# A linear-attention scan followed by a Fourier-mixing block: moving weight conversions, norms and three unread products around the first mixing

## The chip, the cores and the metric

The kernel runs on one core of a Trainium2 chip. The metric is the device time of one execution in microseconds, taken as the median of several runs. The engines are TensorE (PE in the profile, with its weight loads as PEld), VectorE (DVE), ScalarE (ACT), GpSimd (POOL) and SyncE (SP, which here only issues DMAs). Each engine works through its own list of instructions in order and waits on semaphores for the others.

## What is computed

The first half is a delta-rule recurrence over 768 positions for 4 batches of 8 heads with 48 elements each. Its output, laid out as (4, 768, 384), is the input x of the second half.

```
k_n = k / (norm(k) + 1e-6)
for t: y[t] = q[t] @ state
       state += beta[t] * outer(k_n[t], v[t] - k_n[t] @ state)
mixed = real(fft(fft(x, axis=positions), axis=model))
u     = x + mixed
un    = (u - mean(u)) / sqrt(var(u) + 1e-6)
out   = u + relu(un @ w_ch1) @ w_ch2
```

w_ch1 is 384 x 1536 and w_ch2 is 1536 x 384. They arrive as 64-bit floats, and the kernel makes 32-bit floats of them with integer and float operations on ScalarE and VectorE.

## The kernel before

**The scan.** Each batch is cut into six loads of 128 positions, each load into two chunks of 64. A load needs keys turned by TensorE (pre_a, L324), queries turned and multiplied with the keys (pre_q, L533), and the inverse of a small triangular system, which VectorE builds step by step for four loads at once (invert16, L460, in half-size blocks for the first three rounds; invert, L401, later). pre_m16 (L600) joins the half-size inverses: it scales Z on ScalarE, multiplies with the Gram blocks, evicts ND and MT on ScalarE, and makes three further products with a subtraction (Z, L647), an eviction and an addition (MT, L651) between them. step (L680) then carries the state over one chunk, and outputs (L744) gives x.

**The mixing.** folds (L783) adds and subtracts mirrored halves of x on VectorE. fourier (L820) first multiplies the folds with tables over positions (evt, odt), evicts the sums to F, and then, for each of six tiles of 128 rows, multiplies F with the table over the model axis (dtab), evicts one half as Q on ScalarE, adds both halves to x on VectorE, and takes mean and variance. The norms rstd = (var + 1e-6)^(-1/2) are made on GpSimd for two tiles at once (L893 to L897).

**The feed-forward part.** mlp (L900) works on three groups of two tiles. normed_of gives un on VectorE, turned transposes it on TensorE (ptr) and evicts it to unT, first_of makes twelve products ph with w1, each evicted through a Relu to hT by ScalarE, and second_of makes a product po with w2 over twelve pieces and adds it to x. The products ph, po, ptr, the position sums pf and the unread products share one pair of PSUM buffers ("post").

**The weights.** weights (L224) is a generator for both weight matrices, one after the other, each in twelve pieces of 128 x 384. A piece takes two calls: the first issues the ScalarE copy L278, the VectorE mask L279, and for the piece before, the two ScalarE steps L283 and L284; the second issues the VectorE product L291 of an earlier piece, then L295, L299 and L301, and the DMA that stages a later piece. For w1 there are two pairs of working buffers, so the product is that of the piece just before; for w2 three, so it lies two pieces back. w2's stage and working buffers are the fold buffers E and O3 of the first batch. w1's working buffers are those that later hold M (the inverse of round 2, zeroed on GpSimd at L476) and unT.

**The order.** Up to the end of the first mixing the order on PE, DVE, ACT and POOL is written out by hand: advance(gen, n) lets a generator issue up to its n-th next yield, drain lets it issue all the rest. convert(n) calls the conversion n times. In the fifth step of the scan (g = 4) the conversions stand between the state's step and the rest of pre_m16. After the first fourier sums, lines 1273 to 1300 start the feed-forward part; a loop over the twelve first products (L1284) mixes in conversions, the other tiles of the mixing, load 7's pre_m16 (ms[7]), and the remaining key turns (k1 to k3). For the next two loads (period at g = 6 and 7) only PE's order is written out, and the rest is ordered by a scheduler. period (L1002) gives each of its six slots a number of calls to the inversion (inv) and to the conversion (conv) at g = 6:

```python
            if g == NL:
                advance(inv, 4)
                advance(conv, 3 if i < 4 else 4)
```

The function spin (L1099) makes TensorE products that nobody reads; before the change it is called with three and with six, both early in the scan.

Of the kernel before, what the change touches and what calls it, by code (L numbers as in the profile page):

```python
# [64 lines left out]
def kernel(  # L65
# [155 lines left out]
    half_n = const.tile([128, GT], F32, name="half_n")  # L221
    nc.gpsimd.memset(half_n, -0.5)

    def weights():  # L224

        if moe_w_ch1.dtype == F32:
            nc.sync.dma_start(out=w1, in_=moe_w_ch1.rearrange("(c p) f -> p c f", p=128))
            nc.sync.dma_start(out=w2, in_=moe_w_ch2.rearrange("(c p) m -> p c m", p=128))  # L230
            return
        w1v = moe_w_ch1.bitcast(I32).rearrange("(c p) (f two) -> p c f two", p=128, two=2)
        w2v = moe_w_ch2.bitcast(I32).rearrange("(c p) (m two) -> p c m two", p=128, two=2)
        n = DM
        sets = [
            [(w1v[:, :, i:i + 128], w1[:, :, i:i + 128]) for i in range(0, DFF, 128)],
            [(w2v[:, i:i + 1], w2[:, i:i + 1]) for i in range(KF)]]
        for last, pieces in enumerate(sets):
            if last:

                E, O3 = spare.pop()
                ring = E.rearrange("p e t m -> p (e t m)").bitcast(I32).rearrange(
                    "p (i m two) -> p i m two", m=n, two=2)
                tmp = O3.rearrange("p e t m -> p (e t m)").rearrange("p (i e m) -> p i e m", e=2,
                                                                    m=n)
                tmp = [tmp[:, i] for i in range(3)]
                deep = 3
            else:
                ring = wk.tile([128, 4, n, 2], I32, tag="big", bufs=2, name="w64")
                tmp = None  # L250
                deep = 4

            def stage(i):
                if i < len(pieces):
                    src = pieces[i][0]
                    nc.sync.dma_start(
                        out=ring[:, i % deep].rearrange("p (c f) two -> p c f two",
                                                        c=src.shape[1]), in_=src)

            for i in range(deep):  # L260
                stage(i)
            yield
            if tmp is None:
                tmp = [wk.tile([128, 2, n], F32, tag="M", name="wtmp0"),
                       wk.tile([128, 2, n], F32, tag="unT", bufs=2, name="wtmp1")]

            def of(i):
                t = tmp[i % len(tmp)]
                return ring[:, i % deep, :, 0], ring[:, i % deep, :, 1], t[:, 0], t[:, 1].bitcast(I32)


            lag = len(tmp) - 1
            for i in range(len(pieces) + lag):
                if i < len(pieces):
                    lo, hi, man, num = of(i)


                    nc.scalar.activation(man, lo.bitcast(U32), ACT.Copy, scale=2.0 ** -52, bias=1.0)  # L278
                    nc.vector.tensor_scalar(num, hi, 0xFFFFF, None, op0=ALU.bitwise_and)  # L279
                if 0 < i <= len(pieces):  # L280

                    num0 = of(i - 1)[3]
                    nc.scalar.activation(num0, num0, ACT.Relu, scale=-1.0, bias=edges[:, 0:1])  # L283
                    nc.scalar.activation(num0, num0, ACT.Relu, scale=-2.0 ** 23,  # L284
                                         bias=edges[:, 1:2])
                yield
                if i >= lag:
                    _, _, man0, num0 = of(i - lag)
                    dst = pieces[i - lag][1]
                    c = dst.shape[1]  # L290
                    nc.vector.tensor_tensor(dst, man0.rearrange("p (c f) -> p c f", c=c),  # L291
                                            num0.bitcast(F32).rearrange("p (c f) -> p c f", c=c),
                                            op=ALU.mult)
                if i < len(pieces):
                    nc.vector.scalar_tensor_tensor(man, num, 2.0 ** -20, man, op0=ALU.mult,  # L295
                                                   op1=ALU.add)

                    man = man.bitcast(I32)
                    nc.vector.scalar_tensor_tensor(man, hi, -2 ** 31, man, op0=ALU.bitwise_and,  # L299
                                                   op1=ALU.bitwise_or)  # L300
                    nc.vector.tensor_scalar(num, hi, 20, 0x7FF, op0=ALU.logical_shift_right,  # L301
                                            op1=ALU.bitwise_and)
                    stage(i + deep)
                yield
# [515 lines left out]
    def fourier(b):  # L820
# [43 lines left out]
        for T in range(NC):  # L864
# [27 lines left out]
            nc.vector.bn_aggr(mv[:, tt, :], bst)  # L892
            if tt == GT - 1:  # L893
                rstd = wk.tile([128, GT], F32, tag="rstd", bufs=NC // GT, name="rstd")
                nc.gpsimd.tensor_scalar(rstd, mv[:, :, 1], 1e-6, None, op0=ALU.add)
                nc.gpsimd.tensor_tensor(rstd, rstd, half_n, op=ALU.pow)
                norms.append((mv, rstd))  # L897
            yield

    def mlp(b):  # L900
# [24 lines left out]
        def first_of(g):  # L925
            hT = hs[g] = wk.tile([128, KF, GT * 128], F32, tag="big", bufs=2, name="hT")
            for fc in range(KF):
                ph = ps_post([128, GT * 128], "ph")
                for dt in range(KD):
                    mm(ph, w1[:, dt, 128 * fc:128 * fc + 128], un[g][:, dt, :], dt == 0,  # L930
                       dt == KD - 1)
                nc.scalar.activation(hT[:, fc, :], ph, ACT.Relu)  # L932
                yield
# [14 lines left out]
        turns = [normed_of(0), turned(0), first_of(0), normed_of(1)]  # L948
# [3 lines left out]
        else:  # L952
            turns += [second_of(0, 0), turned(1), second_of(0, 1), first_of(1), normed_of(2),
# [48 lines left out]
    def period(g, side):  # L1002
# [48 lines left out]
        for i in range(SLOTS):  # L1051
# [11 lines left out]
            if g == NL:  # L1063
                advance(inv, 4)
                advance(conv, 3 if i < 4 else 4)
# [24 lines left out]
    with tc.manual_schedule(engines=engines):  # L1090
# [6 lines left out]
        unread = ps_post([128, 512], "unread")  # L1097

        def spin(n):  # L1099

            for _ in range(n):
                nc.tensor.matmul(unread[:, 0:DM], lhsT=idle[:, 0:128], rhs=idle, start=True,  # L1102
# [19 lines left out]
        conv = weights()  # L1122
# [12 lines left out]
        spin(6)  # L1135

# [15 lines left out]
        first = part(conv, 2 * KF + 2)  # L1152
        converted = 0
        fold = fd = iter(())

        def convert(n):
            nonlocal converted
            advance(first, n)
            converted += n
# [9 lines left out]
        for g in range(NL - 1):  # L1169
# [22 lines left out]
            else:  # L1192
# [20 lines left out]
                if g > 1:  # L1213
# [4 lines left out]
                fill(3)  # L1218
                if g == 4:
                    advance(n2)  # L1220
                    drain(qs[g + 1])
                    convert(1)
                elif g > 1:
                    convert(1)
                    advance(n2)
                    convert(2 if g == 3 else 1)
                else:
                    advance(n2)
                if g != 4:
# [24 lines left out]
        drain(fd)  # L1254
        drain(keys[0])
        advance(c1)
        late = outputs(g)
# [7 lines left out]
        advance(ms[6])  # L1265
        f = fourier(0)
# [86 lines left out]
```

## Time and profile before

| | |
|---|---|
| median of 3 runs | 754.34 us (752.1 to 760.21) |
| the profiled execution, whole | 761.02 us |
| its span, first to last instruction | 758.9 us |
| TensorE busy | 696.9 us (92% of the span) |
| VectorE busy | 378.6 us (50%) |
| ScalarE busy | 263.7 us (35%) |
| GpSimd busy | 69.7 us (9%) |
| mean granted TensorE clock | 0.953 |

How to read the profile: busy time is summed per engine over the span. Rows of the span in 40 slices give tenths of busy time, and for the clock tenths of full speed. In order of time, a row has its start and length in us, engine, line, operation, tile written, tile read, shape and count, and in brackets the engine's idle time before it with what ended it. A 32-bit matrix product shows as two MATMUL rows, so a count of x6 is three products. The lines below are those of the kernel before.

### The profile page before, as it was taken

What the parts mean: (1) busy time and instruction counts of PE and PEld (TensorE: products, weight loads), DVE (VectorE), ACT (ScalarE), POOL (GpSimd) and SP (SyncE); (2) the same over time, 40 slices, a digit from 0 to 9 for tenths busy, and PEclk for the clock granted to TensorE, in tenths of its full rate; (3) what the DMA queues carried; (4) which work ended last, traced back from release to release, by engine and by line L of the source; (5) the groups of instructions that cost most, each with busy time, mean ns of one, the idle gap of its engine ahead of it and who ended that gap; (6) DMA issues with size and microseconds to landing.
All of it is one profiled execution on the core that took longest, in us unless ns stands there. A gap on an engine that the chain in (4) does not pass through costs nothing.

```text
span 758.9 us, 23039 instructions
## 1 busy us (share of the span) xinstructions
PE 696.9 (92%) x10170; PEld 538.0 (71%) x10170; DVE 378.6 (50%) x957; ACT 263.7 (35%) x644; POOL 69.7 (9%) x114
## 2 busy tenths in 40 slices
PE   6877879598989987999999999999999999999998
PEld 4677868476767655877857767868667678777684
DVE  5867776669932499433198327278512240600000
ACT  5544663568623321223422323223223221211120
POOL 7000000100000011001110210020100110100000
PEclk8698797799999999999999999999999999999999
DMA  9842352014312322002222211001220000000000
GB/s 152 215 74 41 88 135 83 18 54 124 87 29 55 60 44 44 12 11 47 52 45 48 44 34 39 1 13 42 43 44 12 13 12 0 22 1 21 11 10 22
DMA packets 111862, 36.09 MB, mean 48 GB/s; under 512 B 101873, under 2 KB 109842, under 8 KB 111762
## 3 DMA queue, kind: packets, MB, share of 16 engines
q1 hardware_dynamic: 109938, 33.86, 20.5%
q8 instruction: 80, 1.31, 0.7%
q0 software_dynamic: 640, 0.43, 0.4%
q10 hardware_dynamic: 1184, 0.33, 0.3%
q14 instruction: 20, 0.16, 0.1%
HBM read 29.88 MB, written 4.72 MB: 46 GB/s over the span
## 4 chain that ended last, share of the span: by engine, by line
PE 75%; DVE 16%; ACT 5%; issue 2%; DMA 1%; POOL 0%; DVEq 0%; ACTq 0%; POOLq 0%
PE po L110 23%; PE ph L110 21%; PE one L110 16%; PE pair L110 10%; PE one L113 2%; DVE M L452 1%; DVE tmp L448 1%; DVE w L291 1%; PE ptr L113 1%; PE unread L1102 1%; PE pf L110 1%; DMA C<-in_k_dram 1%; DVE M L522 1%; DVE Z L647 1%; DVE tmp L519 1%
## 5 line engine op out<-in xcount | busy, mean ns | idle before, releaser
L110 PE MATMUL ph<-unT,w 128*128 128x256 f32 x864 | 207.7, 392 | 2.8 <-ACT hT L932 2.0
L110 PE MATMUL po<-w,hT 128*128 128x384 f32 x576 | 205.1, 495 | 0.0
L110 PEld LDWEIGHTS ph<-unT,w 128*128 128x128 f32 x864 | 162.4, 194 | 27.6 <-ACT hT L932 2.4
L110 PEld LDWEIGHTS po<-w,hT 128*128 128x128 f32 x576 | 103.7, 190 | 56.7 <-issue 0.3
L932 ACT ACTIVATE hT<-ph 128x256 f32<-128x256 f32 x144 | 54.9, 382 | 145.0 <-PE ph L110 144.9
L943 DVE TENSOR_TENSOR x<-x,po 128x384 f32<-128x384 f32 x24 | 13.2, 550 | 107.0 <-PE po L110 107.0
L741 DVE TENSOR_TENSOR S<-S,pair 128x192 f32<-128x192 f32 x40 | 14.0, 349 | 73.9 <-PE pair L110 73.9
L110 PEld LDWEIGHTS one<-V,MT 64*64 64x64 f32 x768 | 30.5, 141 | 19.5 <-issue 9.2
L884 DVE TENSOR_TENSOR x<-x,one 128x193 f32<-128x193 f32 x24 | 8.5, 354 | 69.8 <-ACT Q L875 69.8
L110 PE MATMUL one<-V,MT 64*64 64x48 f32 x768 | 35.7, 227 | 3.6 <-DVE V L700 1.8
L452 DVE TENSOR_TENSOR M<-M,tmp 128x31 f32<-128x31 f32 (+15 forms) x93 | 34.7, 373 | 3.2
L448 DVE TENSOR_TENSOR tmp<-A,M 128x31 f32<-128x31 f32 (+15 forms) x93 | 34.2, 367 | 2.5
L110 PE MATMUL one<-MT,ND 64*64 64x64 f32 x768 | 30.4, 231 | 5.0 <-DVE x L885 2.6
L110 PEld LDWEIGHTS one<-MT,ND 64*64 64x64 f32 x768 | 27.8, 146 | 6.0 <-ACT Q L875 3.0
L700 DVE TENSOR_TENSOR V<-V,pair 128x192 f32<-128x192 f32 x33 | 11.5, 350 | 38.7 <-PE pair L110 35.4
L110 PEld LDWEIGHTS one<-dtab,F 97*128 97x128 f32 (+1 forms) x192 | 25.2, 191 | 5.2 <-ACT F L879 0.5
L110 PEld LDWEIGHTS pair<-U,K 64*64 64x64 f32 x704 | 16.6, 139 | 17.4 <-issue 14.9
L322 ACT ACTIVATE QT<-one 128x512 f32<-128x512 f32 x24 | 14.3, 594 | 38.9 <-PE one L113 38.7
L110 PE MATMUL one<-dtab,F 97*128 97x97 f32 (+1 forms) x192 | 25.9, 275 | 0.0
L110 PE MATMUL pair<-KT 48*32 48x64 f32 (+1 forms) x1152 | 21.1, 238 | 5.1 <-ACT KT L322 3.8
L110 PEld LDWEIGHTS pair<-S,KT 48*64 48x64 f32 x528 | 10.7, 133 | 20.1 <-issue 10.8
L710 ACT ACTIVATE U<-one 128x192 f32<-128x192 f32 x36 | 11.9, 330 | 37.7 <-PE one L110 37.7
(176 smaller groups left out, 1003.0 us busy)
## 6 DMA issues: line engine op xcount, KB each, us to landing
w<-in_moe_w_ch_dram SPq DMA_DIRECT2D x12, 384.0 KB, 5.6
E<-in_moe_w_ch_dram SPq DMA_DIRECT2D x12, 384.0 KB, 4.3
out_dram<-x SPq DMA_DIRECT2D x24, 192.0 KB, 1.9
K<-in_k_dram SPq DMA_DIRECT2D x92, 48.0 KB, 2.7
V<-in_v_dram SPq DMA_DIRECT2D x92, 48.0 KB, 2.2
C<-in_k_dram SPq DMA_DIRECT2D x18, 192.0 KB, 9.3
Q<-in_q_dram SPq DMA_DIRECT2D x18, 192.0 KB, 3.1
w<-in_q_dram SPq DMA_DIRECT2D x6, 192.0 KB, 7.5
```

The costliest lines, as they stand in the source:

```text
L110: nc.tensor.matmul(o, lhsT=lhsT, rhs=rhs, start=start, stop=stop, skip_group_check=True)
L113: nc.tensor.matmul(o, lhsT=src, rhs=ident[0:src.shape[0], 0:src.shape[0]], is_transpose=True, start=start, stop=True, skip_group_check=True)
L291: nc.vector.tensor_tensor(dst, man0.rearrange("p (c f) -> p c f", c=c), num0.bitcast(F32).rearrange("p (c f) -> p c f", c=c), op=ALU.mult)
L322: nc.scalar.activation(dst.rearrange("p h j t -> p (h j t)"), pt, ACT.Copy)
L448: nc.vector.tensor_tensor(t, A[:, j + 1:W, j:j + 1].broadcast_to([128, n, j + 1]), M[:, j:j + 1, 0:j + 1].broadcast_to([128, n, j + 1]), o ...
L452: nc.vector.tensor_tensor(M[:, j + 1:W, 0:j + 1], M[:, j + 1:W, 0:j + 1], t, op=ALU.add)
L700: nc.vector.tensor_tensor(R4, R4, pw[:, :, 0:2 * D].rearrange("p a (j e) -> p a j e", e=D), op=ALU.subtract)
L710: nc.scalar.activation(U.rearrange("p j e -> p (j e)"), pu[:, 0:4 * D], ACT.Copy)
L741: nc.vector.tensor_tensor(s1v, s0.rearrange("p h j e -> p h (j e)"), pk, op=ALU.add)
L884: nc.vector.tensor_tensor(near, near, pb[:, 0, 0:MH + 1], op=ALU.add)
L932: nc.scalar.activation(hT[:, fc, :], ph, ACT.Relu)
L943: nc.vector.tensor_tensor(x[:, T, :], x[:, T, :], po, op=ALU.add)
```

## The change

1. The generator for both weights becomes weight(last), one for each matrix. w2's first three stage DMAs are issued by the hand-written part ahead of the loop over first products, and w1's remaining calls and w2's are joined by chain(conv, w2s).
2. In the scan's step g = 4, two conversion calls move from ahead of the rest of pre_m16 (and of its subtraction Z) to behind it, and the fold steps there are dropped to be drained later, behind the last chunk's step.
3. In the first mixing, one conversion call no longer stands between the eviction of F and the first Q. ms[7] starts ahead of the position sums. Load 7's first two products of pre_m16 are issued behind the first two mixing tiles, with two unread products between and one after them; they read the table evt.
4. The loop over first products issues two conversion calls behind each product, in place of two behind the first two and one behind the others. The mixing's other tiles are issued at products 1, 3, 6 and 9, not 1, 4, 7 and 10. The query turn for the next load, nq, is issued inside the loop.
5. un of the second group is issued within first_of(0), behind its sixth product, for the first batch; later batches keep their order.
6. The norm rstd is made for each tile by itself: two GpSimd instructions a tile, of one column, for all batches.
7. In period at g = 6, the inversion gets 5 calls a slot instead of 4, and the conversion 2 (4 in the last slot) instead of 3 or 4.

```diff
-    half_n = const.tile([128, GT], F32, name="half_n")
+    half_n = const.tile([128, 1], F32, name="half_n")
...
-    def weights():
+    def weight(last):
...
+        if last:
+            pieces = [(w2v[:, i:i + 1], w2[:, i:i + 1]) for i in range(KF)]
...
+        else:
+            pieces = [(w1v[:, :, i:i + 128], w1[:, :, i:i + 128]) for i in range(0, DFF, 128)]
...
+            if tt == 0:
+                rstd = wk.tile([128, GT], F32, tag="rstd", bufs=NC // GT, name="rstd")
+            rt = rstd[:, tt:tt + 1]
+            nc.gpsimd.tensor_scalar(rt, mv[:, tt, 1:2], 1e-6, None, op0=ALU.add)
+            nc.gpsimd.tensor_tensor(rt, rt, half_n, op=ALU.pow)
             if tt == GT - 1:
-                rstd = wk.tile([128, GT], F32, tag="rstd", bufs=NC // GT, name="rstd")
-                nc.gpsimd.tensor_scalar(rstd, mv[:, :, 1], 1e-6, None, op0=ALU.add)
-                nc.gpsimd.tensor_tensor(rstd, rstd, half_n, op=ALU.pow)
                 norms.append((mv, rstd))
...
                 nc.scalar.activation(hT[:, fc, :], ph, ACT.Relu)
+                if b == 0 and g == 0 and fc == 5:
+                    drain(normed_of(1))
                 yield
...
-        turns = [normed_of(0), turned(0), first_of(0), normed_of(1)]
+        turns = [normed_of(0), turned(0), first_of(0)]
...
-            turns += [second_of(0, 0), turned(1), second_of(0, 1), first_of(1), normed_of(2),
+            turns += [normed_of(1), second_of(0, 0), turned(1), second_of(0, 1), first_of(1), normed_of(2),
...
             if g == NL:
-                advance(inv, 4)
-                advance(conv, 3 if i < 4 else 4)
+                advance(inv, 5)
+                advance(conv, 2 if i < 5 else 4)
...
         def spin(n):
 
+            unread = ps_post([128, 512], "unread")
+            src = idle if idle is not None else evt[:, 0, 0:DM]
             for _ in range(n):
-                nc.tensor.matmul(unread[:, 0:DM], lhsT=idle[:, 0:128], rhs=idle, start=True,
+                nc.tensor.matmul(unread[:, 0:DM], lhsT=src[:, 0:128], rhs=src, start=True,
                                  stop=True, skip_group_check=True)
...
                 fill(3)
-                if g > 1:
+                if g > 1 and g != 4:
                     convert(2)
                 drain(nm)
                 advance(n2)
                 advance(c1)
-                fill(3)
                 if g == 4:
+                    convert(2)
                     advance(n2)
                     drain(qs[g + 1])
                     convert(1)
-                elif g > 1:
-                    convert(1)
+                else:
+                    fill(3)
+                    if g > 1:
+                        convert(1)
                     advance(n2)
-                    convert(2 if g == 3 else 1)
-                else:
-                    advance(n2)
-                if g != 4:
+                    if g > 1:
+                        convert(g - 1)
                     drain(qs[g + 1])
...
-        drain(fd)
         drain(keys[0])
         advance(c1)
+        drain(fd)
...
         advance(ms[6])
+        advance(ms[7])
         f = fourier(0)
         advance(f)
         drain(fold)
         convert(1)
         advance(f, 4)
-        convert(1)
+        w2s = weight(1)
+        advance(w2s)
         advance(f, 2)
         side, done = mlp(0), 0
+        advance(ms[7])
+        convert(1)
+        advance(side)
+        spin(2)
+        advance(ms[7])
+        spin(1)
         advance(side)
         advance(ms[6])
-        advance(ms[7])
-        advance(side)
-        convert(3)
-        advance(ms[7])
-        convert(2)
-
+
+        conv = chain(conv, w2s)
+
+        nq = pre_q(NL)
         k1, k2, k3 = keys[1:]
-        rest = [ms[6], k1, ms[7], k1, ms[7], ms[6], k2, ms[7], k2, ms[7], k3, k3]
+        rest = [k1, ms[7], k1, ms[7], k2, ms[7], k2, k3, nq, k3]
         for fc in range(KF):
-            if converted < 2 * KF + 2:
-                convert(2)
-            else:
-                advance(conv)
             advance(side)
-            if fc % 3 == 1:
+            advance(conv, 2)
+            if fc in (1, 3, 6, 9):
                 advance(f)
-            drain(rest[fc]) if fc == 5 else advance(rest[fc])
+            if fc < len(rest):
+                advance(rest[fc])
         drain(f)
-        nq = pre_q(NL)
-        advance(nq)
         for m in ms[6:] + keys[1:]:
             drain(m)
-        advance(side)
         done = 3 + KF
         inv = invert16(2)
```

## The prediction

> **What bounds the kernel now.** I read the busy slices first, then the order of time on TensorE, then a table of windows.
>
> ```profile
> PE   6877879598989987999999999999999999999998
> ...
> DVE  5867776669932499433198327278512240600000
> ACT  5544663568623321223422323223223221211120
> ...
> PEclk8698797799999999999999999999999999999999
> ```
>
> A slice is 19 us. From slice 16 on TensorE is at 9 nearly everywhere, so the later batches are bound by products that the change leaves alone. Slices 5 to 11 (95 to 228 us) are different: PE falls to 5 to 8, the clock dips, and VectorE stands at 9 to 10 in 9 and 10. The change works there. In order of time on PE, with the idle time and its releaser in brackets:
>
> ```profile
> 130.63 2.03 PE L110 MATMUL one<-dtab,F 97*128 97x97 f32 x16
> 138.56 1.54 PE L113 MATMUL ptr<-pack,un 128*128 128x128 f32 x6 [5.90 <-DVE un L911]
> ...
> 149.22 1.56 PE L110 MATMUL ph<-unT,w 128*128 128x256 f32 x6 [1.98 <-ACT hT L932]
> 153.41 1.15 PE L110 MATMUL one<-MT,ND 64*64 64x64 f32 x32 [2.62 <-DVE x L885]
> ...
> 179.97 0.70 PE L110 MATMUL pair<-QT,KT 48*64 48x64 f32 x32 [2.83 <-ACT QT L322]
> ...
> 183.37 2.86 PE L110 MATMUL ph<-unT,w 128*128 128x256 f32 x12 [0.86 <-ACT unT L922]
> ...
> 212.47 1.11 PE L110 MATMUL pair<-QT,KT 48*64 48x64 f32 x32 [3.34 <-DVE S L741]
> ```
>
> That is 17.5 us of waits. The first is the first mixing's: PE has nothing until two rows of tiles are normed. The next two stand behind a train of conversions on DVE and ACT. The last ends with VectorE's 16-step inversion (its last transpose, L527, ends at 212.2). The train waits on itself, once per conversion of a w1 piece:
>
> ```profile
> 142.49 0.56 DVE L291 TENSOR_TENSOR w<-wtmp 128x384 f32<-128x384 f32 x1 [1.06 <-ACT wtmp L284]
> ...
> 145.71 0.56 DVE L291 TENSOR_TENSOR w<-wtmp 128x384 f32<-128x384 f32 x1 [1.06 <-ACT wtmp L284]
> ```
>
> So a w1 piece takes 3.2 us (1.3 on ACT, then 1.9 on DVE) when nothing lies between. The clock, in windows of 3.41 us (columns: PE, weight loads, DVE, ACT, POOL busy, clock, DMA share, GB/s):
>
> ```profile
> 106.73:110.14 3.41, 1.48 (x55) 1.26 (x50) 3.31 (x9) 0.06 (x1) 0.00 (x0) 1.00 0.40 84
> 110.14:113.55 3.41, 2.81 (x97) 2.49 (x89) 1.51 (x4) 2.65 (x5) 0.00 (x0) 0.50 0.62 149
> ...
> 130.62:134.03 3.41, 2.04 (x17) 1.86 (x16) 0.98 (x4) 2.32 (x6) 0.00 (x0) 1.00 0.70 227
> 134.03:137.45 3.42, 0.00 (x0) 0.00 (x0) 2.71 (x9) 1.12 (x3) 0.40 (x2) 0.50 0.00 0
> ```
>
> The clock halves at 110.14 and stays so to 123.79, again from 134.03 to 144.27, from 154.51 to 157.93 and from 212.54 to 215.95, each time after a thinly used window.
>
> **Part by part.** *Fifth step of the scan (g = 4).* Two conversion steps leave the place ahead of the subtraction Z (L647). In the chain of waits they are L279 0.27, L291 0.47, L295 0.48, L299 0.56, L301 0.27: 2.07 us, and Z starts at 108.32. Its product on PE ends at 106.6, so Z moves to 106.65: 1.7 us. In exchange three fold rows (L805, L808, L810: 1.24 us) go behind the last U (L722). The folds behind that U then sum to 10.1 us (before: 117.41 to 125.84, 8.4). In this profile the window before 110.14 is used for 1.48 of 3.41 us; with Z earlier PE's 1.9 us of idle in it shrink to about 0.7, and I expect the clock to hold. The products between 110.14 and the last U shrink by 2.3 us (full-clock rows: 0.7 for 1.1, 0.65 for 1.1). The last U then comes at 117.4 - 1.7 - 2.3 = 113.4, folds end at 123.5, and the position sums, which wait for the second fold (119) and run 5.2 + 2.8 us, end at 126.9 instead of 130.6: 3.7 us. If the clock falls anyway, or did not fall before, the longer fold tail eats the 1.7: zero. Both ends are kept.
>
> Here a rule of the Trainium skill stands against the trace: "TensorE: Matmul & The Clock Gate", section "HAM oscillation — how this bites in real kernels", puts the limit at idle gaps over some 3.4 us. The longest gap before 110.14 is 1.17 us, and the clock fell. By the rule this edit is worth nothing and the three unread products below are needless; by the rows it is worth 3.7. I go by the rows. The same page's Part 1 says that the window runs freely. Every clock change here is a whole number of 3.41 us after the first one, so the trace agrees, and where a dip falls can differ between executions. That matters for the median below.
>
> *First mixing.* The conversion trio on ACT ahead of the first Q (L278, L283, L284, 1.5 us) goes: the first tile's products end at 131.65, so VectorE's first add starts at 132.0, not 133.05: 1.05 us. rstd per tile (two POOL rows, 0.22 and 0.72 before; one column has no row; between half of that and the same, I take the same) lets one un (0.47) run inside the 1.15 us wait: 0.45. So un is ready at 137.4. PE meanwhile has load 7's first product (1.15 at full clock, 1.97 before), two unread products, load 7's second (1.15), one unread product. An unread one is 128x384: 24 such po rows take 7.75 us in the chain, two rows a product, 0.65. Sum 4.25 us between 132.5 and 137, gated by ND and MT on ACT (1.4 us) and by the release of the first tile's PSUM buffer. They cost nothing while un is later; if un came sooner, at most the last 0.65 shows (1.3 at half clock). The half clock to 144.27 goes (5.7 us of PE work in it: 2.85), and 1.97 of load 7's product no longer stands between ptr and the first product ph. With ptr at 137.0 and two evictions of 0.49, ph starts at 138.5, not 141.93: 3.4 us. With the 3.7: 134.8.
>
> *The loop of 12 first products.* Before, conversion steps stood 22 ahead, 14 in it, 20 calls in the next period; now 17, 24 and 14. Sums for the new loop: DVE 12 conversions x 2.05 + 4 mixing tiles x 1.95 + un, MT, V 2.0 = 34.4 us. ACT 12 x 1.65 + 12 evictions x 0.37 + three key turns with Gram copies 7.6 + Q, mirror (1.75), MT, QT 4.1 = 35.9. PE about 27. The first five iterations are w1's ping-pong: 5 x 3.2 + 2 x 0.95 of mixing that the 1.06 us waits don't cover = 18. The other seven (w2 runs two pieces deep, so no ping-pong) are bound by ACT's remaining 21.6. Together 40 us, to 174.8; before, 34.0, to 175.9. So the conversions moved in here use up what was gained, and PE idles some 13 us in small pieces; windows this thin could again halve the clock once (1.7).
>
> *After the loop.* QT for the next load and un of the second group are now issued inside it. QT's wait (2.83) and most of unT's (0.86) go, and the way from the last ph to the second group's first ph is 2.8 us, not 7.5: 177.6 for 183.37, 5.8 us. Then PE is full up to 209.1, so it reaches the inversion at 203.3.
>
> *The inversion.* VectorE's busy time from un (138.9) to 212.2 is 60.7 us, the same work after. It starts at 137.4 - 3.7 = 133.7, with 5.6 us idle in the loop and 1 elsewhere: 201. ACT's Z and MT take 1.9 more: 203. So PE no longer waits there: 203.3 for 212.47, 9.2 us, and the half clock to 215.95 (3.41 us of PE work: 1.7) goes. Sum 10.9.
>
> *At nothing.* POOL's M memset (L476) now stands ahead of the fourth tile's rstd and waits for the eleventh w1 piece (in this trace the memset follows that L291 directly). The fourth tile's stats come 2 us later, which covers the memset's 0.98; else un and the conversions queued behind it on DVE wait 1 us. 24 more POOL rows lie on an engine 9% busy: per later batch 0.3 us won to 1 lost, I take 0. SP issues the same loads, w2's not later than before; landing is 4 to 6 us, three pieces ahead. Stalls called "issue" (about 1 us each) may shift: 1 us either way.
>
> **The profile's run and the median.** The profiled execution took 761.02 (span 758.9 and 2.1 around it), 6.7 over the median. 761.0 - 10.9 = 750.1 would be an execution as unlucky with the clock. The median one, 754.34, probably has no dip at 110, and then the 3.7 isn't there to win: 754.3 - 7.2 = 747.1; if it has, 743.4. I say 745.
>
> **Rivals.** (1) The loop meets only its ACT sum, 36 us: all later gains grow by up to 4, VectorE's end (197) allows it: 741. For it: mixing rows fill the ping-pong. Against: ACT is in order, and its evictions wait for PE. (2) Within 1%: the loop takes 44 to 46 us, because key turns and evictions (1.3 us an iteration) add to the ping-pong instead of filling it; PE starts the second group at 182 to 184, VectorE ends at 205 to 207, and 1 to 4 us are left: 750.5 to 753. (3) Slower, by one mechanism: two steps behind each product hold ACT so long that every hT eviction is late and PE's two PSUM buffers run dry. The trace has it once: three products from 141.93 to 154.5, 4.2 us each. The break-even is 4.0 us a product (40 us + 7 to 9 us of gains, over 12). At 4.7 us, with half clock in the loop: 758 to 760. Against: the pace of 4.2 had two conversions a product. (4) The filling doesn't hold the clock, since gaps stay before load 7's second product: 2.85 less, 748.
>
> **How the numbers follow.** The main case (743 to 748) 0.47; case 1 0.16; case 2 0.22; case 3 0.07; case 4 0.08. About 1% is what a measurement of this kernel tells from no change: 746.8 and 761.9. Of the main case 0.42 lies below 746.8, of case 4 0.02, and all of case 1: 0.60; slower 0.04 of case 3; the rest within. Range 738 to 753.5: it leaves out the tail of case 1 and most of case 3.
>
> **What would show it.** Clock 1.00 from 124 to 150; the wait of ptr on un short, the un rows 4 us earlier or more; Z of the fifth step right behind its product; the 12 ph groups over 38 to 42 us; no QT wait; no wait of PE behind the inversion. I am wrong if the ph groups lie over 4 us apart, or if PE still waits over 2 us for L527.

## The result and the profile after

The changed kernel takes 750.59 us (median of 20 executions, 748.08 to 755.84). The kernel before, in 20 executions beside it, takes 758.11 (752.1 to 760.42). The ratio is 0.9917, with a 95% interval of 0.9895 to 0.994: about 7.5 us or 0.8% faster. The forecast was 745.0 with a range of 738 to 753.5. The sign and the range hold; the gain is less than forecast, and by the chances given it falls into "within 1%".

The profiled execution of the changed kernel took 754.0 us (span 752.2, mean granted clock 0.964), that of before 761.02 (758.9, 0.953). So from profile to profile 7.0 us are gained where the sum said 10.9. Of the 7.0, 1.7 were there before the first fold row of the fifth step of the scan (102.9 for 104.6). In the profiles of this study that row starts anywhere from 99.5 to 105.6, mostly by where the clock falls earlier on (before 99 us it is halved for 17.1 us in the profile with 99.5, and for 34.1 us in that with 105.6). So below only what comes after the fold row is counted for the change: 5.0 us.

The busy slices of the changed kernel:

```profile
PE   7877879787999986999999999999999999999998
...
DVE  5867777688922699252398128178411241600000
ACT  5544654776414321224422333133223121211120
...
PEclk8798798988999999999999999999999999999999
```

Against before, PE's 5 in slice 7 (132 to 150 us) has become 7 and its 8 in slice 11 a 9, and the clock's two 7s in slices 6 and 7 are 8 and 9. But VectorE still stands at 8, 8 and 9 in slices 8 to 10 (150 to 207 us), and the clock shows 8 in slices 8 and 9, where it had 9. In order of time on PE, with the idle time before a row and its releaser in brackets:

```profile
133.44 0.84 PE L113 MATMUL ptr<-pack,un 128*128 128x128 f32 x6
134.89 1.56 PE L110 MATMUL ph<-unT,w 128*128 128x256 f32 x6 [0.61 <-ACT unT L923]
...
151.39 0.63 PE L113 MATMUL one<-pack,C 128*128 128x128 f32 x4 [4.20 <-ACT O L277]
...
165.22 1.41 PE L110 MATMUL one<-dtab,F 97*128 97x97 f32 x8 [1.76 <-ACT KT L321]
...
172.92 0.69 PE L110 MATMUL pair<-QT,KT 48*64 48x64 f32 x32
...
176.40 1.56 PE L110 MATMUL ph<-unT,w 128*128 128x256 f32 x6
...
186.24 0.59 PE L110 MATMUL pair<-S,KT 48*64 48x48 f32 x16 [2.60 <-DVE S L738]
...
207.37 0.69 PE L110 MATMUL pair<-QT,KT 48*64 48x64 f32 x32 [0.18 <-DVE S L740]
```

The 5.90 us wait ahead of ptr, the 2.83 us wait for QT and the 3.34 us wait behind the inversion are gone. Two others stand in their place: 4.20 us at 151.39 inside the loop, and 2.60 us at 186.24 for the state copy S in the period after it. VectorE in order of time, where it waits or where its queue matters:

```profile
141.94 0.36 DVE L883 TENSOR_TENSOR x<-x,one 128x193 f32<-128x193 f32 x1 [1.28 <-ACT Q L874]
...
143.83 0.53 DVE L290 TENSOR_TENSOR w<-wtmp 128x384 f32<-128x384 f32 x1
...
145.33 0.35 DVE L300 TENSOR_SCALAR wtmp<-w 128x384 int32<-128x384 int32 x1
...
147.01 0.56 DVE L290 TENSOR_TENSOR w<-wtmp 128x384 f32<-128x384 f32 x1 [1.06 <-ACT wtmp L283]
...
148.55 0.35 DVE L300 TENSOR_SCALAR wtmp<-w 128x384 int32<-128x384 int32 x1
150.63 0.36 DVE L883 TENSOR_TENSOR x<-x,one 128x193 f32<-128x193 f32 x1 [1.72 <-ACT Q L874]
150.90 0.35 DVE L884 TENSOR_TENSOR x<-x,one 128x191 f32<-128x191 f32 x1
...
159.63 0.36 DVE L883 TENSOR_TENSOR x<-x,one 128x193 f32<-128x193 f32 x1 [1.28 <-ACT Q L874]
...
169.64 0.36 DVE L883 TENSOR_TENSOR x<-x,one 128x193 f32<-128x193 f32 x1 [1.86 <-ACT Q L874]
...
184.64 0.36 DVE L278 TENSOR_SCALAR O<-E 128x384 int32<-128x384 int32 x1 [1.41 <-DMA E<-in_moe_w_ch_dram]
...
185.84 0.35 DVE L738 COPY S<-pair 128x192 f32<-128x192 f32 x1
...
205.17 1.96 DVE L526 STREAM_TRANSPOSE A<-M 128x1024 f32<-128x1024 f32 x1
```

and ScalarE at the same place:

```profile
148.83 0.39 ACT L933 ACTIVATE hT<-ph 128x256 f32<-128x256 f32 x1
149.09 0.63 ACT L282 ACTIVATE wtmp<-wtmp,edges 128x384 int32<-128x384 int32 x1
149.76 0.61 ACT L283 ACTIVATE wtmp<-wtmp,edges 128x384 int32<-128x384 int32 x1
150.28 0.31 ACT L874 ACTIVATE Q<-one 128x193 f32<-128x193 f32 x1
```

These two are to be read together. VectorE's L300 (148.55) ends one piece's second call. ScalarE's L282 and L283 of the same piece read what it writes and start behind it, at this place also behind an eviction of hT, and Q, whose product on PE ended at 144.6, stands behind them in ScalarE's queue. VectorE then has nothing but the mixing tile to go on with, and that needs Q: 1.72 us idle. The same wait comes at every one of the loop's four tiles: 1.28, 1.72, 1.28 and 1.86 us, 6.1 together. PE's wait at 151.39 comes from this too: the second add (L884) ends at 151.25 and frees the tile's PSUM buffer. The profile names ScalarE's L277 as releaser, but that writes a working buffer of w2, which this product does not touch. With the tile moved, in a later experiment, the same row names L884.

The way of VectorE from the second un to the end of the last inversion transpose, cut at the end of the twelfth first product (columns: us, then busy time of PE, weight loads, DVE, ACT, POOL, clock, DMA share, GB/s):

```profile
133.60:173.00 39.40, 32.39 (x291) 26.43 (x292) 29.93 (x75) 29.75 (x71) 4.40 (x9) 0.87 0.27 71
173.00:207.10 34.10, 30.29 (x338) 23.07 (x338) 30.92 (x93) 19.82 (x44) 2.31 (x4) 0.95 0.29 72
sum 73.50, PE 62.68 PEld 49.50 DVE 60.85 ACT 49.56 POOL 6.71; mean PE 31.34 PEld 24.75 DVE 30.42 ACT 24.78 POOL 3.36
```

VectorE is busy for 60.85 of 73.5 us and idle for 12.7. In the kernel before the same stretch (138.9 to 212.2) is as follows:

```profile
138.90:212.20 73.30, 61.92 (x688) 50.00 (x686) 60.74 (x166) 50.42 (x118) 5.10 (x8) 0.94 0.27 73
```

That is 73.3 us with 60.7 busy and 12.6 idle. The whole train therefore starts earlier, and is as long as it was.

### The profile page after: what moved, and what is told of

Same layout as the page of the kernel before. It is cut to its first block, busy times and chain, and to the rows that moved or that the text cites. A ratio compares the mean times of both kernels' runs of the same rounds, so it can differ in the third digit from the quotient of the medians.

```text
span 752.2 us, 23081 instructions
## 1 busy us (share of the span) xinstructions
PE 695.6 (92%) x10176; PEld 534.9 (71%) x10176; DVE 378.3 (50%) x957; ACT 265.0 (35%) x644; POOL 78.9 (10%) x138
## 4 chain that ended last, share of the span: by engine, by line
PE 76%; DVE 15%; ACT 4%; issue 2%; DMA 1%; POOL 0%; DVEq 0%; ACTq 0%; SPq 0%
PE po L110 23%; PE ph L110 23%; PE one L110 15%; PE pair L110 10%; PE one L113 2%; DVE M L451 1%; DVE tmp L447 1%; PE ptr L113 1%; PE unread L1106 1%; DVE Z L646 1%; DMA C<-in_k_dram 1%; DVE w L290 1%; DVE G L524 1%; DVE A L406 1%; DVE G L455 1%
## 5 line engine op out<-in xcount | busy, mean ns | idle before, releaser
L895 POOL TENSOR_SCALAR rstd<-mv 128x1 f32<-128x1 f32 x24 | 6.4, 266 | 227.1 <-DVE mv L891 227.1
L567 POOL TENSOR_TENSOR MT<-A,pack 128x512 f32<-128x512 f32 x12 | 12.8, 1069 | 130.0 <-PE one L110 64.5
```

Of the source, the lines that this page charges most:

```text
L567: nc.gpsimd.tensor_tensor(MT, MTd[:, m8, None, :].broadcast_to([128, 8, 2, W]), m_blk[:, None, :, None].broadcast_to([128, 8, 2, W]), op=A ...
```

## The experiments

All are edits of the changed kernel, and each ratio is to the kernel before on the same chip. Two theories stood against each other for the missing 5.9 us. One (A) is that VectorE's train from un to the inversion's end sets the time, and that its idle time in the loop comes from where the calls stand. The other (B) is that the time is lost on PE in the period after the loop, where the state copy S stands behind conversions on VectorE.

**Without the three unread products.**

```diff
         advance(side)
-        spin(2)
         advance(ms[7])
-        spin(1)
         advance(side)
```

> The changed kernel without its three unread products in the first mixing; the two products of load 7 stay there. Rows theory (the clock halves after a window of 3.41 us that is thinly used, here under some 60%): PE would be busy some 2.3 us in the 6.7 us from 126.7 to 133.4 behind the dtab products, the clock halves for 7 to 10 us from there on, and the products ph start 1 us later and run slow; the loop behind is bound by ScalarE and VectorE, so at most 1 to 2 us of it reach the end: ratio to before 0.993 to 0.995. Page theory ([...]the longest gap left is about 1.5 us): no change against the changed kernel, 0.9917. If the unread products hold up ptr: faster, 0.990.

Measured: 752.06 us, ratio 0.9927 (0.9902 to 0.9951). This overlaps the changed kernel's interval, so a loss of 1 to 2 us is neither shown nor excluded. In its profile the clock does fall where the products were (windows; columns as above):

```profile
129.50:132.90 3.40, 1.82 (x41) 1.34 (x36) 2.84 (x10) 3.02 (x7) 1.92 (x4) 1.00 0.02 5
132.90:136.30 3.40, 2.53 (x7) 1.86 (x8) 3.34 (x8) 0.92 (x2) 0.00 (x0) 0.50 0.00 0
```

It stays at half to 139.8, and the first ph comes 2.4 us behind ptr instead of 1.5. Since ptr comes sooner without the unread products, the first ph is only 0.3 us later when it is counted from the end of the position sums (9.8 for 9.5 us). The longest gap on PE in the first window is 1.48 us. So here the clock fell where the unread products had held it. They are not needed in every execution, though. In the other profile without them, that of the fastest version below, the window at this place is used a little more, and the clock stays full:

```profile
129.33:132.74 3.41, 2.17 (x38) 1.63 (x38) 2.88 (x9) 2.84 (x6) 1.51 (x3) 1.00 0.00 0
```

What the unread products are worth at the end is too small to be told.

**The scan's fifth step as before.**

```diff
                 fill(3)
-                if g > 1 and g != 4:
+                if g > 1:
                     convert(2)
...
                 advance(c1)
+                fill(3)
                 if g == 4:
-                    convert(2)
                     advance(n2)
...
                 else:
-                    fill(3)
                     if g > 1:
...
+        drain(fd)
         drain(keys[0])
         advance(c1)
-        drain(fd)
```

> The changed kernel with the order of the scan's step g = 4 and of the folds set back to that of before; all else as changed. My prediction gave this part 3.7 us on the path to the first mixing. If all of it reaches the end: 0.9966. Theory that VectorE's list sets the point where TensorE meets the inversion (207.1 us in the profile): the sums start some 3.7 us later, VectorE starts its list later by the same, and nothing behind has slack to take it up: 0.995 to 0.997. Rival, that the state copy's wait and the clock behind it (186 us) are what sets that point: part of the 3.7 is taken up, 0.993.

Measured: 751.44 us, ratio 0.991 (0.9876 to 0.9943), no difference from the changed kernel that can be told. From the U ahead of the fold rows to the end of the position sums in pf its profile has 24.9 us, the kernel before 25.0 and the changed kernel 22.7. In these profiles the step thus gains 2.2 us and not 3.7. That isn't a fixed size: over all profiles of this study the stretch takes 22.2 to 24.5 us in the ten with the new order and 22.9 to 25.0 us in the three with the old one, with the clock at half for 0 to 10.2 us of it in the new and 10.2 to 13.7 us in the old. By the medians nothing of it can be seen at the end.

**The state copy on ScalarE.**

```diff
-            if begin:
+            if begin and b == 1:
+                nc.scalar.activation(s1v, pk, ACT.Copy)
+            elif begin:
                 nc.vector.tensor_copy(s1v, pk)
```

> The changed kernel, with the first state of the second batch copied out of PSUM by ScalarE instead of VectorE, nothing else moved. It takes away the wait of 2.6 us that TensorE has at 186.24 us for that copy, and with it perhaps the half clock of 3.4 us behind it. Theory A (VectorE's list, which ends its inversion at 207.1, sets the point): TensorE gets there 3 to 4 us sooner and waits there instead; at most 0.5 us gained from one row less on VectorE: 0.991 to 0.992. Theory B (TensorE's wait and its clock set the point): 3 to 4.3 us gained, 0.986 to 0.988.

Measured: 751.8 us, ratio 0.9912 (0.988 to 0.9943): no gain. The copy comes at 178.3, 7.5 us earlier, and PE waits further on instead:

```profile
187.95 0.67 PE L110 MATMUL one<-V,MT 64*64 64x48 f32 x16 [2.92 <-DVE V L699]
```

V is a subtraction that VectorE makes, in the same queue as the conversions. The copy is the place at which PE meets VectorE's lateness, not its cause. Theory B falls as an explanation of the missing time.

**The period's split as before.**

```diff
             if g == NL:
-                advance(inv, 5)
-                advance(conv, 2 if i < 5 else 4)
+                advance(inv, 4)
+                advance(conv, 3 if i < 4 else 4)
```

> The changed kernel with the calls of the first period as before: 4 of the inversion in each slot, 3 of the conversion (4 in the last two), so that the conversions end earlier and the inversion later. Theory A: VectorE has the same rows in another order; the state copy is no later, but the inversion is drained in one piece later: within 1 us of the changed kernel, 0.990 to 0.993. Theory B: the state copy stands behind three conversion calls a slot, not two, TensorE waits longer for it, 1 to 2 us lost: 0.993 to 0.995.

Measured: 755.0 us (22 executions), ratio 0.997 (0.9951 to 0.999), whose interval lies above that of the changed kernel: some 4 us of the gain hang on this part, more than either theory gave. In its profile the wait for the state copy grows from 2.60 to 4.57 us:

```profile
186.67 0.68 PE L110 MATMUL pair<-S,KT 48*64 48x48 f32 x16 [4.57 <-DVE S L738]
```

That is the mechanism of theory B. The changed kernel's profile is a poor partner for it, since the clock halves once more in its loop. The profile with the scan's step as before has a loop of the same length (34.8 us), and this row:

```profile
182.46 0.45 PE L110 MATMUL pair<-S,KT 48*64 48x48 f32 x16 [2.38 <-DVE S L738]
```

Against it the wait is 2.2 us longer, the half clock behind it lasts 6.8 us and not 3.4, and PE is at the inversion 73.4 us behind the first ph and not 70.0. That is most of the 4 us. But from the first ph to the end the two profiles take 617.1 and 616.3 us (the changed kernel 617.3), so that this reaches the end is not shown by them, only by the medians.

**The norm for two tiles at once.**

```diff
-    half_n = const.tile([128, 1], F32, name="half_n")
+    half_n = const.tile([128, GT], F32, name="half_n")
...
-            if tt == 0:
-                rstd = wk.tile([128, GT], F32, tag="rstd", bufs=NC // GT, name="rstd")
-            rt = rstd[:, tt:tt + 1]
-            nc.gpsimd.tensor_scalar(rt, mv[:, tt, 1:2], 1e-6, None, op0=ALU.add)
-            nc.gpsimd.tensor_tensor(rt, rt, half_n, op=ALU.pow)
             if tt == GT - 1:
+                rstd = wk.tile([128, GT], F32, tag="rstd", bufs=NC // GT, name="rstd")
+                nc.gpsimd.tensor_scalar(rstd, mv[:, :, 1], 1e-6, None, op0=ALU.add)
+                nc.gpsimd.tensor_tensor(rstd, rstd, half_n, op=ALU.pow)
```

> The changed kernel with rstd made for two tiles at once, as before. My prediction gave the split 0.45 us in the first mixing and nothing elsewhere: 0.992. If the GpSimd rows that the split adds cost the later batches something (up to 1 us each): 0.989 to 0.990.

Measured: 750.5 us, ratio 0.9922 (0.99 to 0.9944): no difference. In the changed kernel the second un waits 0.47 us for rstd where the two of before wait 1.15; from the end of the position sums to the first ph the profile without the split has 9.9 us and the changed kernel 9.5. So the 0.45 priced for this is there, and is below what the medians can tell.

**The mixing tile between the two conversion calls.** Two calls behind one another are the second half of one piece and the first half of the next. With the tile between them, Q stands ahead of the next L282 and L283, and VectorE has the tile to do while these run.

```diff
             advance(side)
-            advance(conv, 2)
+            advance(conv)
             if fc in (1, 3, 6, 9):
                 advance(f)
+            advance(conv)
```

> The changed kernel; in the loop over first products the mixing's tile is issued between the two conversion calls, not behind both. In the changed kernel each Q on ScalarE stands behind the conversion pair L282, L283, which waits for VectorE's L300, so VectorE waits 1.3 to 1.9 us for Q in each of four tiles (6.1 us), and TensorE's next key turn waits 4.2 us for the tile's PSUM buffer, after which the clock halves. Theory A (VectorE's list sets the end, and its idle time in the loop is this order): VectorE's idle time between the second un and its last transpose falls from 12.6 to 8 or 9 us, the wait of 4.2 us at the key turn goes; 2 to 4 us gained, 0.986 to 0.989. Rival C (VectorE's waits only move to the conversions' own ping-pong): same as the changed kernel, 0.991 to 0.993.

Measured: 745.37 us, ratio 0.9852 (0.9813 to 0.9891), below the changed kernel's interval: 5.2 us by the medians, with the same work, and more than the 2 to 4 us of theory A. (The kernel before takes 758.06 us on this chip, and 758.11 on that of the changed kernel.) VectorE in order of time, at the places where it had waited:

```profile
144.68 0.56 DVE L290 TENSOR_TENSOR w<-wtmp 128x384 f32<-128x384 f32 x1 [0.20 <-ACT wtmp L283]
...
147.90 0.56 DVE L290 TENSOR_TENSOR w<-wtmp 128x384 f32<-128x384 f32 x1 [1.06 <-ACT wtmp L283]
...
150.37 0.36 DVE L883 TENSOR_TENSOR x<-x,one 128x193 f32<-128x193 f32 x1 [0.57 <-ACT Q L874]
...
166.42 0.36 DVE L883 TENSOR_TENSOR x<-x,one 128x193 f32<-128x193 f32 x1 [0.55 <-ACT Q L874]
```

PE at the key turn and at the state copy:

```profile
151.13 0.63 PE L113 MATMUL one<-pack,C 128*128 128x128 f32 x4 [1.96 <-DVE x L884]
...
180.22 0.45 PE L110 MATMUL pair<-S,KT 48*64 48x48 f32 x16 [0.99 <-DVE S L738]
```

And the windows from the second un to the last transpose, cut as above:

```profile
135.60:168.10 32.50, 27.43 (x290) 22.94 (x288) 27.83 (x72) 27.07 (x65) 3.85 (x9) 1.00 0.34 83
168.10:201.00 32.90, 28.81 (x339) 21.98 (x338) 32.38 (x95) 21.74 (x51) 2.47 (x4) 1.00 0.31 78
sum 65.40, PE 56.23 PEld 44.92 DVE 60.22 ACT 48.81 POOL 6.32; mean PE 28.12 PEld 22.46 DVE 30.11 ACT 24.41 POOL 3.16
```

VectorE's busy time is the same, 60.2 us, and its idle time 5.2 instead of 12.7. The waits for Q are 1.1 us together, not 6.1, PE's wait at the key turn has halved (and its releaser is now named as the add), the wait for the state copy has shrunk along with it, and the clock stays at 1.00 through the stretch. This is theory A: the idle time came from the place of the calls, and it set the end. One rival is left, that the clock made the gain; the next profile answers it.

**That, and the state copy on ScalarE.** The edit of the third experiment on top.

> The step before with the first state of the second batch copied by ScalarE as well. Theory A: TensorE's wait for the state (2.6 us) comes to matter only now that VectorE ends sooner: 1 to 2 us better than the step before, 0.984 to 0.988. If TensorE waits for VectorE's next row (V, L699) instead, as it did when only the copy was moved: no change against the step before.

Measured: 743.94 us (741.32 to 746.2), ratio 0.9836 (0.9797 to 0.9875), the fastest kernel of this study. PE's wait for V behind the copy is now short:

```profile
180.61 0.67 PE L110 MATMUL one<-V,MT 64*64 64x48 f32 x16 [0.52 <-DVE V L699]
```

That it is 1.4 us better than the version without the copy lies within the intervals.

This kernel and that of the third experiment differ by the place of the call alone, and in both profiles the clock halves twice for 3.41 us on VectorE's way from the second un to the last transpose, once of it in the loop. The third experiment's windows, cut as above, and then this one's:

```profile
133.70:169.80 36.10, 29.12 (x290) 24.22 (x290) 26.63 (x69) 27.69 (x65) 4.41 (x9) 0.95 0.29 75
169.80:205.56 35.76, 30.70 (x336) 22.86 (x338) 33.68 (x97) 21.86 (x52) 2.38 (x4) 0.95 0.29 71
...
131.62:164.15 32.53, 29.14 (x290) 24.14 (x290) 27.87 (x73) 27.10 (x65) 3.84 (x9) 0.95 0.31 84
164.15:197.33 33.18, 30.40 (x339) 23.13 (x338) 32.23 (x94) 21.40 (x52) 2.89 (x4) 0.95 0.29 76
```

At the same clock VectorE's work is 60.3 and 60.1 us, its idle time 11.6 and 5.6 us, and PE is at the inversion 70.9 and 64.7 us behind the first ph. So the place of the call, and not the clock, gives the 6 us, and with the step before it theory A is shown.

**Less work on VectorE.** The step that sets w2's sign (L298) is left out, so that VectorE has less to do and the order stays as it is.

```diff
-                nc.vector.scalar_tensor_tensor(man, hi, -2 ** 31, man, op0=ALU.bitwise_and,
-                                               op1=ALU.bitwise_or)
+                if not last:
+                    nc.vector.scalar_tensor_tensor(man, hi, -2 ** 31, man, op0=ALU.bitwise_and,
+                                                   op1=ALU.bitwise_or)
```

> The changed kernel, with w2's conversion leaving out the sign (L298, 12 rows of 0.56 us on VectorE: 5.6 to 6.7 us of its list), so that w2 is taken without its sign. Theory A: VectorE's last transpose comes 5 to 6 us earlier, TensorE is then bound by its own products behind the second group's start, and 3 to 5 us are gained: 0.985 to 0.988. Theory B' (TensorE sets the point by its products from 186 us on, VectorE just keeps up): the state copy still comes earlier by 2 to 3 us; 2 to 3 us gained, 0.988 to 0.989. Neither (ScalarE sets it): no change, 0.9917.

Measured: 746.34 us, ratio 0.9873 (0.983 to 0.9917), 4.3 us less than the changed kernel by the medians. VectorE's train has 55.4 us of work for 60.9, with 11.7 idle, so 5.5 us less of work gave about 4. This agrees with a stretch that VectorE bounds. It doesn't show it by itself, since the two intervals overlap between 0.9895 and 0.9917.

**The fastest version with single parts changed back or moved on.** Three kernels on top of the tile between the calls and the copy on ScalarE: the scan's fifth step as before; without the unread products; and F's mirrored half of the first batch (L879 of the changed kernel) copied by GpSimd instead of ScalarE:

```diff
-                    nc.scalar.activation(F[0:n, i, HALF + 1:SEQ], F[0:n, i, HALF - 1:0:-1],
-                                         ACT.Copy)
+                    if b:
+                        nc.scalar.activation(F[0:n, i, HALF + 1:SEQ], F[0:n, i, HALF - 1:0:-1],
+                                             ACT.Copy)
+                    else:
+                        nc.gpsimd.tensor_copy(F[0:n, i, HALF + 1:SEQ], F[0:n, i, HALF - 1:0:-1])
```

> The kernel with the tile between the conversion calls and the state on ScalarE, but with the scan's step g = 4 and the folds in the order of before. In the changed kernel this part was worth nothing that could be told. If that was because VectorE's idle time in the loop took up any gain ahead of it, it must show now: VectorE starts its list up to 2 us later and has only 5.6 us of idle time left; 1 to 3 us lost, ratio to before 0.985 to 0.988. If the part is worth nothing by itself (the longer fold tail eats Z's earlier start): 0.983 to 0.985.

> The same kernel without the three unread products. The clock halved for 6.8 us in the first mixing when they were left out of the changed kernel, and the first product ph came 1 us later behind ptr. If the loop is bound by VectorE and ScalarE, some 1 us reaches the end: 0.984 to 0.986. If the half clock delays evictions and so the conversions: 2 to 3 us, 0.986 to 0.988. If they are not needed: 0.983.

> The same kernel with the mirror copy of F (four rows, 1.75 us on ScalarE in the loop's second product) made by GpSimd for the first batch. Theory A (ScalarE's queue delays VectorE's conversions there): up to 1 us gained, 0.982 to 0.983. If GpSimd takes over 3 us for it, the fourth tile's dtab products wait, and nothing or 1 to 2 us is lost: 0.984 to 0.986.

Measured: 745.85 (ratio 0.9842, 0.981 to 0.9874), 744.92 (0.9856, 0.9827 to 0.9886) and 745.4 (0.9846, 0.981 to 0.9883). None can be told from 0.9836. GpSimd takes 2.30 us for the mirror copy, and the un of the second group starts 17.7 us behind the end of the first group's with it and 18.0 without. The scan's part and the unread products remain worth less than the measurement can tell, also where VectorE's train waits less.

## Why the prediction was right or wrong

**First mixing: right.** From the end of the position sums in pf to the first ph it took 12.6 us and now takes 9.5: 3.1 gained for 3.4 predicted, and the split of the norm shows its 0.45. The clock stays full from 118.1 to 152.3. That ph starts at 134.9 for 134.8 predicted is partly luck: counted from the fold row it comes 5.3 us earlier, not 7.1, and most of the difference is the scan's.

**Fifth step of the scan: half right.** Z stands 2.5 us behind the U ahead of the folds, not 3.9: 1.4 us for 1.7 predicted. "I expect the clock to hold" failed: the clock halves from 111.3 to 118.1, behind a window in which PE was busy for 1.70 of 3.42 us. So the 2.3 us by which the products were to shrink mostly stayed away, and the step gives 2.2 in this pair of profiles instead of 3.7.

**The loop: right in length, by luck. QT: right.** The twelve first products take 38.1 us (38 to 42 given), QT's wait is gone, and the thirteenth starts at 176.4 for 177.6 predicted. The one dip of the clock that was allowed for came as two, 152.3 to 155.7 and 165.9 to 172.7; in profiles with one dip fewer the loop takes 34.8 us. That is some 5 us less than the 39.6 of the sum (18 + 21.6), and only the second, longer dip brought the loop into the range. Nor was in the loop what the sum had put there, as the next paragraph says.

**The inversion: wrong, and here the gain went.** The step that failed reads: "It starts at 137.4 - 3.7 = 133.7, with 5.6 us idle in the loop and 1 elsewhere: 201." The start is right (the second un ends at 133.6) and so is the work (60.85 us for 60.7). The idle time is 12.7, not 6.6, and the last transpose ends at 207.1. I had found the loop's idle time as a difference of sums, 40 - 34.4, on the assumption that mixing rows fill the waits of the conversions. They could not, since Q stood behind L282 and L283. VectorE did 29.9 us of work in the loop and not 34.4, and idled 9.5 there; the work left over went into the next period, whose 34.1 us had 3.2 idle. The loop's share is the order's: it is 9.4 to 9.5 us also in the three profiles whose loop takes 34.8 us. The 3.2 hangs on the clock as well: it is 1.2 and 2.1 us in the two of these that keep the period's split. Putting the tile between the calls, and nothing else, brought the idle time to 5.2 and the time to 745.37.

**"Then PE is full up to 209.1": wrong, as a consequence.** From 176.4 to the first po (201.0) PE takes 24.7 us for what I had put at about 19.6. It waits 2.60 us for the state copy, behind VectorE's L278, which waited 1.41 us for a piece of w2, and the clock halves from 186.4 to 189.8. With PE late as well, the wait behind the inversion is gone as predicted (0.18), but because both come at 207. PE gets there, counted from the fold row, 3.4 us sooner, not 9.2. The half clock behind it (212.5 to 216.0 before) is gone, 1.6 us for 1.7 predicted. Together they make the 5.0.

**The base: wrong.** I took the median of three, 754.34, for an execution without the dip at 110, and forecast from it. Twenty executions have their median at 758.11, so the three were a lucky draw, and the profiled one (761.02) was less out of the way than I said. Had I subtracted 10.9 from 758.1, the forecast would have been 747.2. Against the median that it started from, 754.34, the forecast was a gain of 9.3, between the 10.9 and the 7.2 of an execution without the dip; 7.5 came. That 9.3 lies nearer to it than 10.9 does is owed to this mix and not to the working.

**Of the rivals**, the second comes nearest: 1 to 4 us at the inversion (3.4 measured), VectorE's end at 205 to 207 (207.1), 750.5 to 753 (750.6). Its mechanism, a loop of 44 to 46 us, is not what happened. The third (late evictions of hT, so that PE's PSUM buffers run dry) is not it either: the one wait of PE for hT that the loop's rows show is 0.44 us, and the 4.20 us is a wait for a PSUM buffer that VectorE's add frees. The first and the fourth did not come: VectorE ends at 207.1 and not at 197, and the clock held through the first mixing.

## What to carry to other kernels

Where two engines hand a job back and forth in order, other work may fail to fill their waits until it is put between the halves on both queues: look at what stands ahead of the shared step on each engine, not at the sums of busy time. In this kernel one call moved by one place was worth 5.2 us, beside 7.5 us for the whole change. And a wait that PE shows for a small copy (here S) may only be the place at which it meets a late engine: moving the copy moved the wait to V.

## What the runs showed of the hardware

**The clock falls without a long gap.** It halved at 111.3 in the changed kernel, after a window with PE busy 1.70 of 3.42 us and no gap above 1.41 us; and in the kernel without unread products after 1.82 of 3.40 with none above 1.48. The Trainium skill, "TensorE: Matmul & The Clock Gate", section "HAM oscillation — how this bites in real kernels", asks for gaps over some 3.4 us, and these traces don't agree with it. What the traces show is the used share of a window. All clock changes of a profile lie on one grid of 3.41 us. Over the thirteen profiles, a window of this grid at full clock with PE busy for less than 40% of it was followed by half clock in 32 of 32 cases, one with 40 to 70% in 61 of 185, and one with more in none of 2412. Two pairs of windows of the changed kernel; in each the first is at full clock and thinly used, and the second is at half:

```profile
107.89:111.31 3.42, 1.70 (x95) 1.45 (x90) 2.62 (x7) 2.52 (x5) 0.00 (x0) 1.00 0.36 65
111.31:114.72 3.41, 2.93 (x108) 2.74 (x99) 1.83 (x5) 1.83 (x6) 0.00 (x0) 0.50 0.52 140
...
182.98:186.40 3.42, 0.82 (x13) 0.40 (x14) 2.01 (x9) 2.18 (x5) 0.00 (x0) 1.00 0.68 208
186.40:189.81 3.41, 3.41 (x23) 2.78 (x20) 3.41 (x13) 1.43 (x4) 0.00 (x0) 0.50 0.45 121
```

Between 40 and 70% the share alone doesn't decide, and what does is open.

**Executions differ, and the clock goes with it.** Twenty executions of the kernel before span 752.1 to 760.42 us, and twenty of the changed one 748.08 to 755.84. Of 42 more of the kernel before, the slowest (763.53 us) has a mean granted clock of 0.946 and the fastest (753.79 us) one of 0.964. For a change of 1%, three executions don't give the base.

**A load that may delay another in SP's queue.** The piece of w2 that VectorE waited for at 184.64 was issued by SP at 181.19, 0.17 us after a K load issued at 180.42 had ended (0.60 us), which itself had been held for PE. That this hold is the cause was read from the trace and not tried.
